# A fused sliding-window attention and gated FFN on one core: seven-product outputs for five tiles instead of two, half-sums formed in place

## The chip, the cores and the metric

One core of a Trainium2 chip. The engines are TensorE (PE, with its weight loads PEld), VectorE (DVE), ScalarE (ACT), GpSimd (POOL) and SyncE (SP), which issues DMAs. The metric is the device time of one launch in microseconds, the median over several runs. The kernel is built with a tile framework that inserts the semaphores; the order of instructions on each engine is the order in which the program emits them.

## The reference

```python
# attention: q, k, v are (8, 8, 576, 64): batch, head, position, head dimension
scores = (1 / sqrt(64)) * matmul(q, k.transpose(0, 1, 3, 2))
mask = (rel >= 0) & (rel < 64)                    # rel = query position - key position
attn = softmax(where(mask, scores, -1e9))
x = matmul(attn, v).transpose(0, 2, 1, 3).reshape(4608, 512)
# gated feed-forward: w_gate and w_val are (512, 1536), w_out is (1536, 512)
out = (maximum(x @ w_gate, 0) * (x @ w_val)) @ w_out
```

## The kernel before

**Tiles.** The 4608 tokens are cut into ten tiles: 0 to 3 of 384 tokens, 4 to 9 of 512 (`NS = 4`, `LAST = 9`). For a wide tile t the program emits a hidden layer (`fast_hidden`) and then an output layer. Between the pieces of tile t's output stand the value products of tile t+1 (`values`: PE products, then on VectorE reciprocal, normalisation and a 32x32-block transpose, "turn") and the scores of tile t+2 (`scores`: PE products, exponentials on ScalarE, masks on VectorE). So attention work runs one and two tiles ahead.

**Seven products.** The hidden layer multiplies 2x2 blocks with seven products instead of eight (Winograd's form). P1 to P7 are accumulated in PSUM banks that ScalarE copies ("snap", "seed") and VectorE adds. For this the kernel needs block differences of the weights, formed once (`us`, `vs`), and of x, formed per tile by `x_form` into `xc` (four per tile: on VectorE up to tile 4, on GpSimd from tile 5 on). A hidden layer works on three groups j = 0, 1, 2 of features.

**Outputs.** Tiles 2 to 6 and 9 use `fast_output`: 48 matmuls of 512 columns for a wide tile. Tiles 7 and 8 (`FAST_OUT`) use `SevenOut`: seven products of 12 matmuls with 256 columns each. These need four half-sums of g, the gated hidden layer (`g_form`, index n = 0 to 3, in three pieces j), and four differences of w_out (`o_form`, 12 instructions). The half-sums of pieces 0 and 1 with n = 0, 1 are made by GpSimd during the hidden layer; of the last piece by VectorE, followed by n = 2 for all pieces on VectorE and n = 3 on GpSimd (behind a small copy, L679, that makes GpSimd wait for VectorE). Their results lie in memory of other tiles that is no longer used: `nats` (raw q and k), `qTs[0]`, `kTs[0]`. P5 uses n = 0, P6 n = 1, P7 n = 2, P3 n = 3.

**Order.** A planner, `Weaver`, holds a clock in estimated microseconds and a heap of due events: `W.at(time, fn)` plans an emission, `W.advance(t)` emits all that is due. PE work advances the clock. An engine's queue is in order and doesn't wait for the planner's time, only for semaphores; the planned time sets the place in the queue. `bank()` hands out one of eight PSUM banks and waits (in the plan) until one is free. Before P3 the add of P7 must have read its bank.

**Loads.** q and k come in by GpSimd-issued DMAs (`qk_load`, batch b) into `nats` and are transposed on VectorE (`qk_trans`, 4 per batch) at planned times within tile t for the scores of tile t+2, which stand at the end of tile t's output; v comes in by GpSimd-issued DMAs (`v_load`) and is copied between partitions by SP-issued ones (`v_spread`). `ahead(t)` plans them for tiles t+2 and t+3, relative to T (the start of tile t) and `ends` (T + 32.7 for a wide tile).

The order within the output of a seven-product tile is a tuple, v for values, s for scores, h for the first product of the next hidden layer:

```python
SEVEN = {-2: ("v0", "P2", "v1", "P6", "P5", "P7", "s0", "P4", "s1", "P3"),
         -1: ("v0", "P2", "P6", "v1", "P7", "P5", "P4", "h1", "P3")}
```

Of the kernel before, what the change touches and what calls it, by code (L numbers as in the profile page):

```python
# [47 lines left out]
def kernel(  # L48
# [10 lines left out]
    nc = tc.nc  # L59
# [31 lines left out]

    wg = persist.tile([128, NC, DF], FP16)
# [219 lines left out]

    def u_pv(u, hhs=(0, 1), banks=None):

        d = units[u]
        if "pv" not in d:
            if u >= 6:
                d["pv"] = [bank() for _ in range(2)]
                unread.update(map(id, d["pv"]))
            elif banks:  # L320
                d["pv"] = [one_bank() for _ in range(2)]
            else:
                d["pv"] = two_banks()
# [12 lines left out]
        return 0.27 * len(hhs)  # L336
# [11 lines left out]
    def u_norm(u, hh):  # L348

        d = units[u]  # L350
        if "x" not in d:
            d["x"] = a_n.tile([128, 2, SB, 2, D // 2], FP16, name="x")
        nc.vector.tensor_tensor(d["x"][:, hh], pv_of(d, u, hh)[:, :, 0:D].rearrange("p s (c e) -> p s e c", e=2),
                                d["r"][:, hh, :, :, None].to_broadcast([128, SB, 2, D // 2]), MUL)
        if u >= 6:
            read(d["pv"][hh], True)

    def u_norm_act(u, hh):

        d = units[u]  # L360
        if "x" not in d:
            d["x"] = a_n.tile([128, 2, SB, 2, D // 2], FP16, name="x")
# [120 lines left out]
    def t_turn(t, hh):  # L483
        dst = xt_tile(t)[:, 2 * hh:2 * hh + 2].rearrange("p e (s c) -> p s e c", c=32)
        nc.vector.transpose(dst, wides[t]["x"][:, hh])

    xcs = {}

    def x_form(t, n):

        HT = widths[t] // 2
        if t not in xcs:
            xcs[t] = x_sb.tile([128, 4, 2, WT // 2], FP16, name="xc", tag="xt")
        xt, xc = xt_tile(t), xcs[t][:, :, :, 0:HT]
        b11, b12, b21, b22 = (xt[:, 2 * k:2 * k + 2, HT * h:HT * h + HT] for k in range(2) for h in range(2))
        x, y = ((b12, b11), (b22, xc[:, 0]), (b22, b12), (b21, xc[:, 1]))[n]
        (nc.vector if t <= NS else nc.gpsimd).tensor_tensor(xc[:, n], x, y, SUB)
        if n == 3:
            normed[0] = t

    def values(t, hh, T, banks=None, give=False):
# [87 lines left out]
    def fast_hidden(t, seven=None):  # L589
# [4 lines left out]
        xt, xc = xt_tile(t), xcs[t][:, :, :, 0:HT]  # L594
# [60 lines left out]
        def add(j, name, i, n, delay):  # L655

            def summed():
# [11 lines left out]
                else:  # L669
                    def product_of():  # L670
                        late = seven and j == last
                        mult(nc.vector if late else nc.gpsimd, j, n, 1, pr[:, 0], pr[:, 1])
                        if seven and n == 0:
                            for s in range(2):
                                g_form(nc.vector if late else nc.gpsimd, t, s, j)
                            if late:
                                for jj in range(3):
                                    g_form(nc.vector, t, 2, jj)
                                nc.gpsimd.tensor_copy(last2[0:1], gsums[2][0:1, HF - 1, 0:2])  # L679
                                for jj in (2, 0, 1):  # L680
                                    g_form(nc.gpsimd, t, 3, jj)
# [57 lines left out]
    def fast_output(t, between):  # L739
# [3 lines left out]
        for sub, before in enumerate(between):  # L743
# [13 lines left out]
            def evac(op=op, sub=sub):  # L757
# [7 lines left out]
    wts = persist.tile([128, 3, HF, QN], FP16)  # L765
    wos = {(k, n): wo[:, HF * k:HF * k + HF, QN * n:QN * n + QN] for k in range(2) for n in range(2)}
    gsums = [nats.rearrange("p a n -> p (a n)")[:, HF * QN * i:HF * QN * i + HF * QN].rearrange("p (f n) -> p f n", f=HF)
             for i in range(3)]
    dead = [tile_.rearrange("p a s c -> p (a s c)")[:, 0:HF * QN].rearrange("p (f n) -> p f n", f=HF)
            for tile_ in (qTs[0], kTs[0])]  # L770
    gsums.append(dead[0])
    wts_ = [dead[1]] + [wts[:, i] for i in range(3)]

    def o_form(eng, n, j):

        c = slice(2 * j, 2 * j + 2)
        to = wts_[n][:, c]
        b11, b12, b21, b22 = (wos[k, m][:, c] for k in range(2) for m in range(2))
        x, y, op = ((b12, b11, SUB), (wts_[2][:, c], b11, ADD), (b22, b12, SUB), (b21, wts_[1][:, c], SUB))[n]
        eng.tensor_tensor(to, x, y, op)  # L780

    def g_form(eng, t, n, j):
# [5 lines left out]
        x, y, op = ((a21, a22, ADD), (gsums[0][:, c], a11, SUB), (a11, a21, SUB), (a12, gsums[1][:, c], SUB))[n]  # L788
        eng.tensor_tensor(gsums[n][:, c], x, y, op)  # L789
        gs[t][1]["sum", n, j] = True  # L790

    class SevenOut:
# [8 lines left out]
        def product(self, name):  # L801
# [10 lines left out]
            f0, h, n = {"P1": (0, 0, None), "P2": (HF, 0, None), "P4": (HF, 1, None)}.get(name, (0, 0, None))  # L812
            s = {"P5": 0, "P6": 1, "P7": 2, "P3": 3}.get(name)
            B = {"P1": wos[0, 0], "P2": wos[1, 0], "P3": wos[1, 1], "P4": wts_[3],
                 "P5": wts_[0], "P6": wts_[1], "P7": wts_[2]}[name]
            for c0, c1 in ((0, 4), (4, 6)):
                for m in range(2):
                    W.advance(W.clock)
                    for c in range(c0, c1):
                        while (("sum", s, c // 2) if s is not None else (f0 + c, h)) not in done:  # L820
                            W.pop()
                        A = gsums[s][:, c] if s is not None else g_sb[:, f0 + c, 256 * h:256 * h + 256]
# [48 lines left out]
        def do_P2(self):  # L871
            self.evac("B", 0, 0)

# [48 lines left out]
    def output_last(t):  # L922
# [3 lines left out]
        for c0, c1, queue in ((0, 256, nc.sync), (256, 384, nc.sync), (384, DM, nc.scalar)):  # L926
# [4 lines left out]
            o_sb = consts.tile([128, c1 - c0], FP32, name=f"o_last{c0}")  # L931
            nc.scalar.copy(o_sb, op[:, 0:c1 - c0])
            queue.dma_start(out[bass.ds(starts[t] + last * 128, 128), c0:c1], o_sb)

    SEVEN_LAST = ("P6", "P5", "P2", "P7", "oP1", "P3", "P4")
    SEVEN = {-2: ("v0", "P2", "v1", "P6", "P5", "P7", "s0", "P4", "s1", "P3"),
             -1: ("v0", "P2", "P6", "v1", "P7", "P5", "P4", "h1", "P3")}

    with tc.manual_schedule():
# [12 lines left out]
        zero32 = consts.tile([128, 384], FP32)  # L952
# [120 lines left out]
        LAST = NS + NL - 1  # L1073
        FAST_OUT = (LAST - 2, LAST - 1)
# [12 lines left out]
        def ahead(t):  # L1087
# [17 lines left out]
        def begin(t):  # L1105
            if t not in running:
                ready(t)
# [19 lines left out]
        for t in range(2, NS + NL):  # L1127
            ready(t)
            ahead(t)
            begin(t)  # L1130
            if t in FAST_OUT:
                seven = sevens[t]
                if t == FAST_OUT[0]:
                    for j in range(3):
                        W.at(W.clock + 0.5, lambda j=j: o_form(nc.gpsimd, 0, j))
# [12 lines left out]
            if t == FAST_OUT[0] - 1:  # L1148
                for i, n in enumerate((2, 1, 3)):
                    for j in range(3):  # L1150
                        W.at(W.clock + 10 + 0.1 * (3 * i + j), lambda n=n, j=j: o_form(nc.gpsimd, n, j))
# [48 lines left out]
```

## Time and profile before

| what | value |
|---|---|
| median of 3 runs | 312.11 us (311.72 to 312.48) |
| profiled execution, its own time | 312.83 us |
| its span, first to last instruction | 311.1 us |
| granted TensorE clock | 1.000 of full speed |
| tile 2 and tile 3, hidden start to hidden start | 24.58 and 26.59 us |
| tile 9, from its second group of products to the end | 30.95 us |
| GpSimd TENSOR_TENSOR `g_sb<-pr`, 128x512, f32 to f16 (mean) | 1.27 us |
| GpSimd TENSOR_TENSOR `nats<-g_sb`, 128x512 f16 (mean) | 1.15 us |
| VectorE TENSOR_TENSOR `pr<-bank,pr`, 128x512 f32 (mean) | 0.68 us |
| VectorE transposes of q, k and of x (mean) | 1.25 us |
| loads of v (128 KB) and of q (288 KB), issue to landing | 5.5 and 7.2 us |

The span starts with the first instruction of any engine. A row of the profile's groups or timeline names the engine, the line of the program, the operation, then what is written and read; "x3" counts instructions, and what stands in brackets is idle time before it and what ended it. Where a helper issues an instruction, the helper's line stands there: L625 is every hidden product, L754 the normal output, L823 the seven-product output, L431 the masks, L497 the x differences, L789 the half-sums of g, L780 the differences of w_out, L198 the transposes of q and k, L485 those of x, L479 the normalisation, L650 the products of gate and value, L661 the adds in the hidden layer, L864 the adds in the output.

### The profile page before, as it was taken

The numbers are of one execution on the slowest core, as the hardware profiler recorded it, in microseconds if no ns is written. First come the engines' busy times: TensorE is split into PE (matmuls) and PEld (weight loads), VectorE is DVE, ScalarE is ACT, GpSimd is POOL, SyncE is SP. The second block draws the span as 40 slices with busy tenths as digits, with TensorE's granted clock in tenths as the row PEclk, the third lists the DMA queues.
The fourth block names the chain that finished last, engine by engine and source line by source line (L and its number), as shares of the span: only waits on it lengthen the run. The fifth ranks groups of instructions, "written<-read, shape, count | busy, mean of one in ns | idle before, by whom it ended". The sixth has DMA issues, their size and how long they took to land.

```text
span 311.1 us, 10718 instructions
## 1 busy us (share of the span) xinstructions
PE 297.2 (96%) x4511; PEld 226.6 (73%) x4511; DVE 239.8 (77%) x460; ACT 198.1 (64%) x410; POOL 194.1 (62%) x222
## 2 busy tenths in 40 slices
PE   4899989999999998999999999999999999999996
PEld 2575878449958955885588558855888788878854
DVE  5937976987997999689868986898559986885540
ACT  3645348158858845982888278837885688537842
POOL 8768689849930491237924792999873927483430
PEclk9999999999999999999999999999999999999999
DMA  7999996999994189304990399011910210012012
GB/s 218 183 196 205 194 193 104 135 194 165 75 187 131 39 140 188 76 0 66 223 154 1 44 231 158 7 36 70 152 32 16 69 59 0 3 55 84 1 37 101
DMA packets 57169, 32.84 MB, mean 106 GB/s; under 512 B 39456, under 2 KB 49568, under 8 KB 57120
## 3 DMA queue, kind: packets, MB, share of 16 engines
q0 software_dynamic: 46688, 18.29, 50.1%
q1 hardware_dynamic: 10288, 13.80, 14.0%
q8 instruction: 35, 0.57, 0.7%
q14 instruction: 14, 0.11, 0.1%
q10 hardware_dynamic: 144, 0.07, 0.1%
HBM read 37.75 MB, written 9.44 MB: 152 GB/s over the span
## 4 chain that ended last, share of the span: by engine, by line
PE 79%; DVE 7%; DMA 5%; POOL 4%; issue 3%; ACT 1%; DVEq 0%; POOLq 0%
PE bank L625 42%; PE bank L754 18%; PE bank L897 5%; PE bank L580 5%; PE bank L264 3%; DMA wg<-in_moe_w_gate_dram 3%; PE bank L823 2%; DMA v<-in_v_dram 2%; PE bank L460 2%; DVE xw L479 1%; POOL v L204 1%; DVE nats L789 1%; PE bank L332 1%; DVE g_sb L650 1%; PE bank L929 1%
## 5 line engine op out<-in xcount | busy, mean ns | idle before, releaser
L650 POOL TENSOR_TENSOR g_sb<-pr 128x512 f16<-128x512 f32 (+1 forms) x44 | 52.6, 1206 | 74.9 <-ACT pr L667 73.3
L661 DVE TENSOR_TENSOR pr<-bank,pr 128x512 f32<-128x512 f32 (+1 forms) x96 | 58.6, 650 | 4.8 <-PE bank L625 3.3
L754 PE MATMUL bank<-wo,g_sb 128*128 128x512 f16 x252 | 58.0, 380 | 1.3 <-issue 1.3
L644 ACT COPY pr<-bank 128x512 f32<-128x512 f32 (+1 forms) x96 | 49.3, 567 | 14.5 <-PE bank L625 14.1
L650 DVE TENSOR_TENSOR g_sb<-r,bank 128x512 f16<-128x512 f32 (+1 forms) x48 | 31.4, 653 | 29.4 <-ACT r L690 22.6
L754 PEld LDWEIGHTS <-g_sb 128*128 128x128 f16 x252 | 23.2, 98 | 27.7 <-issue 1.9
L625 PE MATMUL bank<-xc,vs 128*128 128x256 f16 (+1 forms) x288 | 41.3, 266 | 0.1
L625 PE MATMUL bank<-xc,us 128*128 128x256 f16 (+1 forms) x288 | 41.3, 266 | 0.0
L625 PEld LDWEIGHTS <-vs 128*128 128x128 f16 x384 | 36.5, 98 | 3.9 <-issue 0.4
L625 PEld LDWEIGHTS <-us 128*128 128x128 f16 x384 | 36.5, 98 | 3.3
L204 POOL DMA_DIRECT2D v<-in_v_dram x41 | 34.7, 864 | 1.7 <-DMA nats<-in_q_dram 1.0
L759 ACT COPY o_sb<-bank 128x512 f32<-128x512 f32 x21 | 12.3, 587 | 32.6 <-PE bank L754 30.6
L431 DVE TENSOR_TENSOR pw<-pw,mask 128x512 f16<-128x512 f16 x48 | 28.6, 633 | 5.2 <-ACT pw L426 4.4
L667 ACT ACTIVATE pr<-pr 128x512 f32<-128x512 f32 (+1 forms) x48 | 29.2, 608 | 4.7 <-DVE pr L661 4.7
L690 ACT ACTIVATE r<-bank 128x512 f32<-128x512 f32 (+1 forms) x48 | 27.8, 579 | 5.6 <-PE bank L625 5.4
L625 PEld LDWEIGHTS <-wg 128*128 128x128 f16 x288 | 27.4, 98 | 3.9 <-issue 0.2
L625 PEld LDWEIGHTS <-wv 128*128 128x128 f16 x288 | 27.4, 98 | 2.5
L625 PE MATMUL bank<-xt,wv 128*128 128x256 f16 (+1 forms) x192 | 27.5, 266 | 0.0
L625 PE MATMUL bank<-xt,wg 128*128 128x256 f16 (+1 forms) x192 | 27.5, 266 | 0.0
L426 ACT ACTIVATE pw<-bank 128x512 f16<-128x512 f32 x48 | 24.9, 605 | 1.8 <-PE bank L264 1.2
L634 ACT COPY bank<-bank 128x512 f32<-128x512 f32 (+1 forms) x48 | 24.9, 553 | 0.6 <-PE bank L625 0.4
L563 ACT ACTIVATE pr<-bank 128x384 f32<-128x384 f32 x24 | 11.5, 493 | 16.2 <-PE bank L580 13.2
(106 smaller groups left out, 517.2 us busy)
## 6 DMA issues: line engine op xcount, KB each, us to landing
out_dram<-o_sb SPq DMA_DIRECT2D x35, 256.0 KB, 3.3
nats<-in_k_dram POOLq DMA_DIRECT2D x15, 288.0 KB, 5.3
nats<-in_q_dram POOLq DMA_DIRECT2D x15, 288.0 KB, 7.2
v<-in_v_dram POOLq DMA_DIRECT2D x31, 128.0 KB, 5.5
v<-v SPq DMA_DIRECT2D x12, 132.0 KB, 2.5
v<-v SPq DMA_DIRECT2D x24, 66.0 KB, 2.1
wg<-in_moe_w_gate_dram POOLq DMA_DIRECT2D x6, 256.0 KB, 6.5
wv<-in_moe_w_val_dram POOLq DMA_DIRECT2D x6, 256.0 KB, 8.3
```

The costliest lines, as they stand in the source:

```text
L204: nc.gpsimd.dma_start(v16s[b % 2][lo:hi, g, :, 0:64], v[b, :, 64 * g - 64 + lo:64 * g - 64 + hi].rearrange("h p d -> p h d"))
L426: nc.scalar.activation(d["p"][g].rearrange("p n c -> p (n c)"), d["st"][g], ACT.Exp, scale=scale)
L431: nc.vector.tensor_tensor(d["p"][g], d["p"][g], mask[:, None, :].to_broadcast([128, 2 * QW, 64]), MUL)
L580: nc.tensor.matmul(h[:, b * n:b * n + n], wt[:, c, (f + b) * 128:(f + b) * 128 + 128], xt[:, c, c0:c0 + n], start=(c == 0), stop=(c == NC ...
L625: nc.tensor.matmul(to[:, HT * m:HT * m + HT], w[:, k, 128 * m:128 * m + 128], x[:, k], start=(first and m == 0 and k == 0), stop=(k == 1), ...
L634: nc.scalar.copy(at[j, "B", i][:, 0:TW], at[j, "A", i][:, 0:TW])
L644: nc.scalar.copy(pr[:, i], at[j, "A", i][:, 0:TW])
L650: eng.tensor_tensor(gh[:, f:f + 2, h], pair(r), pair(v), MUL)
L661: nc.vector.tensor_tensor(pr[:, i], to[:, 0:TW], pr[:, i], ADD)
L667: nc.scalar.activation(pr[:, 0], pr[:, 0], ACT.Relu)
L690: nc.scalar.activation(r, to[:, 0:TW], ACT.Relu)
L754: nc.tensor.matmul(op, g_sb[:, f, 128 * sub:128 * sub + 128], wo[:, f], start=(i == 0), stop=(i == NF - 1))
```

## The change

Five tiles (4 to 8) use `SevenOut` instead of two. The half-sums of g no longer need four buffers: n = 0 is written over a block of g, n = 2 and n = 3 over others, and only n = 1 has a buffer of its own, `s2`, which shares memory with the x tile of the narrow tiles (`xus`). The differences of w_out get four buffers of their own and are formed by GpSimd in tiles 3 and 4 (six each) instead of 6 and 7. In tiles 4 to 7 VectorE makes n = 2 of the last piece only and GpSimd the other two; n = 3 follows on GpSimd, planned behind P2. The x differences of tiles 5 to 9 move from GpSimd to VectorE and are planned together behind P4. P5 takes the bank that has been free longest. Transposes of q and k, loads of q, k and v get other planned times; GpSimd waits at two places for masks (`behind_quad`). In tile 8 the second turn is planned 0.8 us later and the next tile's first product no longer waits in the plan for the x differences.

```diff
+    xus = persist.tile([128, 2, 2, U // 32 * D], FP16)
...
+    def behind_quad(qd):
+        nc.gpsimd.tensor_copy(last[0:1], quads[qd]["p"][G - 1][0:1, QW, 0:2])
...
-        (nc.vector if t <= NS else nc.gpsimd).tensor_tensor(xc[:, n], x, y, SUB)
+        (nc.vector if t <= NS or t - 1 in FAST_OUT else nc.gpsimd).tensor_tensor(xc[:, n], x, y, SUB)
...
-    def values(t, hh, T, banks=None, give=False):
+    def values(t, hh, T, banks=None, give=False, turn=2.7):
...
-        W.at(T + 0.7, lambda: t_recip(t, hh))
+        W.at(T + (1.15 if give else 0.7), lambda: t_recip(t, hh))
...
-        W.at(T + 2.7, lambda: t_turn(t, hh))
-        for n, x in (((0, 4.0),), ((1, 4.0), (2, 4.1), (3, 5.0)))[hh]:
+        W.at(T + turn, lambda: t_turn(t, hh))
+        for n, x in (((0, 4.0),), ((1, 4.0), (2, 4.1), (3, 5.0)))[hh] if not give else ():
...
                             if late:
-                                for jj in range(3):
+                                masks = t + 2 <= LAST
+                                for jj in (j,) if masks else range(3):
                                     g_form(nc.vector, t, 2, jj)
-                                nc.gpsimd.tensor_copy(last2[0:1], gsums[2][0:1, HF - 1, 0:2])
-                                for jj in (2, 0, 1):
-                                    g_form(nc.gpsimd, t, 3, jj)
+                                nc.gpsimd.tensor_copy(last2[0:1], g_sb[0:1, HF - 1, 0:2])
+                                for jj in range(2) if masks else ():
+                                    g_form(nc.gpsimd, t, 2, jj)
...
-    wts = persist.tile([128, 3, HF, QN], FP16)
+    wts = persist.tile([128, 4, HF, QN], FP16)
...
+    s2 = xus.rearrange("p a h n -> p (a h n)")[:, 0:HF * QN].rearrange("p (f n) -> p f n", f=HF)
...
-        x, y, op = ((a21, a22, ADD), (gsums[0][:, c], a11, SUB), (a11, a21, SUB), (a12, gsums[1][:, c], SUB))[n]
-        eng.tensor_tensor(gsums[n][:, c], x, y, op)
+        to, x, y, op = ((a21, a21, a22, ADD), (s2[:, c], a21, a11, SUB), (a11, a22, s2[:, c], SUB), (a12, a12, s2[:, c], SUB))[n]
+        eng.tensor_tensor(to, x, y, op)
...
-                at[self.TO[name]] = bank()
+                at[self.TO[name]] = bank(0, name == "P5")
...
         def do_P2(self):
             self.evac("B", 0, 0)
+            for j in range(3):
+
+                def formed(j=j):
+                    while ("sum", 2, 2) not in gs[self.t][1]:
+                        W.pop()
+                    g_form(nc.gpsimd, self.t, 3, j)
+                W.at(W.clock + 1.0, formed)
...
+    FAST_OUT = (LAST - 5, LAST - 4, LAST - 3, LAST - 2, LAST - 1)
+    O_FORMS = {3: [(1.5 + 0.1 * j, 2, j) for j in range(3)] + [(1.8, 0, 0), (6.5, 0, 1), (9.0, 0, 2)],
+               4: [(2.5 + 0.1 * i, n, j) for i, (n, j) in enumerate((n, j) for n in (1, 3) for j in range(3))]}
+    LATE, VAT, QAT = (6.0, 8.0, 10.7, 14.2), 1.0, 4.0
+    XAT = -0.3
...
-                qk_turns(t + 2, T, (0.1, 1.4, 8.0, 14.2) if long else (0.1, 1.4, 6.1, 10.7))
-                v_ahead(t + 2, ends, ends - 5.0 if long else T + 3.0 if t == 2 else ends + 0.5)
+                qk_turns(t + 2, T, LATE if t - 1 in FAST_OUT else (0.1, 1.4, 8.0, 14.2) if long else (0.1, 1.4, 6.1, 10.7))
+                v_ahead(t + 2, ends, ends + VAT if t in FAST_OUT else ends - 5.0 if long else T + 3.0 if t == 2 else ends + 1.5)
+                if t + 1 == NS:
+                    W.at(ends + 1.4, lambda: behind_quad(3))
             if t + 3 <= LAST:
-                qk_loads(t + 3, ends - 11.0)
+                qk_loads(t + 3, ends - (QAT if t in FAST_OUT else 11.0))
...
+            if t == 3:
+                behind_quad(1)
+            for T, n, j in O_FORMS.get(t, ()):
+                W.at(W.clock + T, lambda n=n, j=j: o_form(nc.gpsimd, n, j))
             if t in FAST_OUT:
...
                     if name[0] == "v":
-                        values(t + 1, int(name[1]), W.clock, [bank(0, True) for _ in range(3)], True)
+                        values(t + 1, int(name[1]), W.clock, [bank(0, True) for _ in range(3)], True,
+                               3.5 if t == LAST - 1 else 2.7)
...
                     elif name[0] == "h":
+                        while ("turned", 0) not in wides[t + 1]:
+                            W.pop()
                         begin(t + 1)
                     else:
                         seven.product(name)
+                        if name == "P4":
+                            for n in range(4):
+                                W.at(W.clock + XAT + 0.05 * n, lambda n=n: x_form(t + 1, n))
```

More of the change, by code (lines that the diff above doesn't have):

```diff
@@ L361, in u_norm_act @@
         if "x" not in d:
-            d["x"] = a_n.tile([128, 2, SB, 2, D // 2], FP16, name="x")
+            d["x"] = xus[:, u % 2].rearrange("p h (s e c) -> p h s e c", e=2, c=D // 2)
         pv = pv_of(d, u, hh)
@@ L764 @@
     QN = DM // 2
-    wts = persist.tile([128, 3, HF, QN], FP16)
+    wts = persist.tile([128, 4, HF, QN], FP16)
     wos = {(k, n): wo[:, HF * k:HF * k + HF, QN * n:QN * n + QN] for k in range(2) for n in range(2)}
[L767 to L772, printed above, removed]
+    s2 = xus.rearrange("p a h n -> p (a h n)")[:, 0:HF * QN].rearrange("p (f n) -> p f n", f=HF)
     def o_form(eng, n, j):
         c = slice(2 * j, 2 * j + 2)
-        to = wts_[n][:, c]
+        to = wts[:, n, c]
         b11, b12, b21, b22 = (wos[k, m][:, c] for k in range(2) for m in range(2))
-        x, y, op = ((b12, b11, SUB), (wts_[2][:, c], b11, ADD), (b22, b12, SUB), (b21, wts_[1][:, c], SUB))[n]
+        x, y, op = ((b12, b11, SUB), (wts[:, 2, c], b11, ADD), (b22, b12, SUB), (b21, wts[:, 1, c], SUB))[n]
         eng.tensor_tensor(to, x, y, op)
@@ L821, in product @@
                             W.pop()
-                        A = gsums[s][:, c] if s is not None else g_sb[:, f0 + c, 256 * h:256 * h + 256]
+                        A = s2[:, c] if name == "P6" else g_sb[:, f0 + c, 256 * h:256 * h + 256]
                         nc.tensor.matmul(to[:, QN * m:QN * m + QN], A[:, 128 * m:128 * m + 128], B[:, c],
@@ L951 @@
             v_fixed(i, nc.vector)
-        zero32 = consts.tile([128, 384], FP32)
+        zero32 = wts.rearrange("p a f n -> p (a f n)").bitcast(FP32)[:, 0:384]
         nc.vector.memset(zero32, 0.0)
```

36 lines of the change are left out of this document (16 added, 20 removed).

## The prediction, written before the changed kernel was run

> **What bounds the kernel now.** I read the page's busy times and its chain of waits first, to learn which engine sets the end.
>
> ```profile
> PE 297.2 (96%) x4511; PEld 226.6 (73%) x4511; DVE 239.8 (77%) x460; ACT 198.1 (64%) x410; POOL 194.1 (62%) x222
> PE 79%; DVE 7%; DMA 5%; POOL 4%; issue 3%; ACT 1%; DVEq 0%; POOLq 0%
> L754 PE MATMUL bank<-wo,g_sb 128*128 128x512 f16 x252 | 58.0, 380 | 1.3 <-issue 1.3
> ```
>
> TensorE sets the end; only fewer columns on it, or fewer holes, can shorten the run. The next view is the table by stage, one row per 512-row tile, cut where the chain starts the next tile's hidden layer (tiles 4 to 8; the last row also holds 0.87 us of tile 9's first products).
>
> ```profile
> 122.31:154.02 31.71, 31.71 (x474) 23.21 (x473) 26.64 (x45) 22.05 (x42) 17.22 (x17) 1.00 0.44 96
> 154.02:185.74 31.72, 31.72 (x475) 23.23 (x473) 26.66 (x45) 22.06 (x42) 18.96 (x20) 1.00 0.69 108
> 185.74:217.50 31.76, 31.76 (x474) 23.25 (x473) 26.78 (x44) 22.06 (x42) 25.48 (x24) 1.00 0.46 71
> 217.50:249.00 31.50, 30.95 (x511) 26.76 (x509) 23.93 (x43) 22.32 (x43) 23.05 (x23) 1.00 0.47 67
> 249.00:280.15 31.15, 30.33 (x390) 26.41 (x389) 24.52 (x48) 20.53 (x39) 17.50 (x16) 1.00 0.09 29
> ```
>
> The columns are length, then busy time of PE, PE's loads, DVE, ACT and POOL. Tiles 4 to 6 have no hole on PE and give DVE 26.7 us of work in 31.7. Tile 7, which has the seven products already, is only 0.26 shorter than tile 6. The last view is the timeline of tile 7's output, and beside it what a mask costs next to GpSimd.
>
> ```profile
> 239.32 0.42 DVE L789 TENSOR_TENSOR nats<-g_sb 128x512 f16<-128x512 f16 x1
> 240.13 1.08 DVE L789 TENSOR_TENSOR nats<-g_sb 128x512 f16<-128x512 f16 x3
> 241.13 1.34 DVE L479 TENSOR_TENSOR xw<-bank,rw 128x128 f16<-128x128 f32 x3
> 241.41 3.37 POOL L789 TENSOR_TENSOR qT<-g_sb,nats 128x512 f16<-128x512 f16 x3
> 241.47 1.47 PE L823 MATMUL bank<-kT,nats 128*128 128x256 f16 x12 [0.21 <-DVE xw L479]
> 246.85 4.34 DVE L431 TENSOR_TENSOR pw<-pw,mask 128x512 f16<-128x512 f16 x5
> 278.68 1.47 PE L823 MATMUL bank<-wo,qT 128*128 128x256 f16 x12 [0.59 <-DVE o_sb L864]
> 148.91 1.33 POOL L497 TENSOR_TENSOR xc<-xt 128x512 f16<-128x512 f16 x1
> 151.49 4.26 POOL L204 DMA_DIRECT2D v<-in_v_dram  x5
> L431 DVE TENSOR_TENSOR pw<-pw,mask 128x512 f16<-128x512 f16 x2 | 2.7, 1371 | 0.0
> L431 DVE TENSOR_TENSOR pw<-pw,mask 128x512 f16<-128x512 f16 x2 | 0.8, 424 | 0.1
> 252.88 0.69 DVE L650 TENSOR_TENSOR g_sb<-r,bank 128x512 f16<-128x512 f32 x1
> ```
>
> The two mask rows are from 149.8 to 150.6, with GpSimd's x differences running, and from 152.8 to 153.5, with GpSimd only issuing loads of v: 1.37 us against 0.42. An fp16 operation of VectorE on two SBUF tiles costs 0.95 more beside a GpSimd sum and nothing more beside GpSimd's DMA issues.
>
> **The products, part one.** A normal wide output is 48 matmuls of 512 columns; the chain has 2.70 us for 12, so 10.80. Seven products are 84 of 256 columns; the chain has 1.31 for 12, so 9.17. Each of tiles 4, 5 and 6 could give 1.63, 4.9 together. Tile 7 shows how much of it stays. In PE starts, from its P1 (233.93) to tile 8's first product (248.84) there are 14.91 us; work in it is 9.17 for products, 1.75 for four hidden pieces (0.436 each), 1.24 for two value and 1.24 for two score groups, together 13.40. 1.5 us are holes. So the question is what the new order does to the holes.
>
> **The output phase redrawn, on tile 7's times.** (1) VectorE formed five half-sums from 239.32 to 241.21; now it forms three (two of index 0 and 1, one of index 2), so it is free at 240.55, 0.66 earlier. Normalisation and turns, which follow, move up by as much: the first value bank comes free 0.6 earlier. (2) P5 waited from 241.08 to 241.47 for such a bank; it now takes the longest-free bank and need not wait. It ends at 242.4. (3) New wait: P7 needs the index-2 sums of the other two pieces, made by GpSimd behind a small copy that waits for VectorE (0.17, as at 241.27). At 1.13 each (3.37 for three) they end at about 243.0; P7's first matmuls can start on piece 0, so about 0.4 is lost. Queued behind P7 on PE are the scores. (4) Those needed a normalised bank at 244.53; it is now free by 243.98, when P7 ends at 244.16, so that hole of 0.4 closes. (5) P4 and the second scores follow; the latter still wait some 0.25 for the third exponential. (6) P3 needs the index-3 sums; GpSimd makes them right behind, 243.0 to 246.4, and P3 starts at 247.2. It needs the add of P7 too: VectorE's second turn ends near 245.7, the add 246.3. P3 ends at 248.5 instead of 248.84: **0.35 saved**, a stage of 31.15.
>
> The form of these sums is new: they write into strided g. Nearest rows are 1.15 (strided source) and 1.27 (the fp32 multiplication into g) on GpSimd; below, 1.12. I take 1.13 because sizes and type are those of the first. At 1.27, P7 is 0.25 later per tile, 1.2 over five tiles; at 1.12 nothing changes.
>
> **x differences.** Four leave GpSimd (1.25 each, 244.75 to 250.24) for VectorE, where tile 4's took 0.42, spaced 0.34. In the new order they come behind P7's add and one mask, from about 246.7, when GpSimd's sums end at 246.4. Uncontended they cost VectorE 1.5. The eight masks gain: before, five took 0.87 each beside GpSimd's differences; now most take 0.42. VectorE's queue (add, 4 differences, 8 masks, last add) ends about 3.2 us into the next tile; before it ended 3.9 in, and the first gate product was due right then (252.88, against 249.00). Cover left: 0.7. Bounds for the four: 1.4 to 5.5; I take 1.5.
>
> **Tiles 4 to 6** carry what tile 7 does not: four transposes of 1.22 (4.9). VectorE had 26.7 there; two late multiplications (1.25), three half-sums (1.15), two adds (1.25) and four differences (1.5) add 5.15, uncontended masks take off some 2.5 (5.1 to 6.5 before, 3.3 at 0.42): 29.3 in a stage of 31.15. It fits, with 6% to spare. The moved transposes (6.0, 8.0, 10.7, 14.2 us) fall into idle times of tile 7's hidden layer of 0.69, 1.13, 0.43 and 2.02; so gate products slip by up to 1.75 and catch up by the last slot. The banks they free are wanted about as late; I put 0.1 on it, bounds 0 and 1.2.
>
> Tile 4 is worse. GpSimd now waits there for the masks (about 122.2), then issues v loads (4.3) and makes six weight differences (1.16 each) until 133.5, so its first multiplication slips from 129.6 to 133.5 and its sums end at 143.1, under VectorE's first late multiplication. I add 0.4. The six differences in tile 3 lie in its idle GpSimd time (12.8 us before 101.31). Later q and k loads (four issues of 0.56) and v loads (0.86 each) come right behind the index-3 sums, land some 7 us after, and are first needed 6 us into the next tile; GpSimd's first multiplication is due at 7.2, so they cost nothing unless that cover of about 2 us goes. SP's v copies wait for them, but the next store is due 21 us into the tile.
>
> **Tile 8.** P3 waited from 277.93 to 278.68 for P7's add, which stood behind a 1.25 us turn. That turn now comes at 3.5 instead of 2.7, behind the add: **0.75 saved**. The differences follow the turn, the first by 279.05, and tile 9 wants it at 279.24. Without it 0 is saved.
>
> **Sum.** Tile 4 0.2, tile 5 0.5, tile 6 0.5, tile 7 0.35, tile 8 0.75: 2.3 us. The profiled execution took 312.83 (span 311.1 and 1.7 around it), so it would be 310.5; the median of the runs is 0.72 lower, so **309.8**. One stall I leave at zero: 1.31 us at 116.45 in tile 3, which the profile puts down to nothing, while DMA queues were full and v loads were being issued. These loads now come 9 us later; the stall may go, or another may appear elsewhere: plus or minus 1.3.
>
> **Rivals.** *More is regained.* The redrawing is pessimistic: holes close in all five tiles. Against 13.40 of work, another half microsecond in each and the stall at 116.45 gone gives 2.3 + 2.5 + 1.3 = 6.1, so 306.0. For it: bank holes were what tile 7 mostly showed. Against it: P7's new wait.
>
> *GpSimd's sums meet VectorE's differences: slower.* If the index-3 sums run 0.7 us or more later than drawn, differences and masks run beside them. Three caught operations cost 3 x 0.95 = 2.85; less the cover of 0.7, the first gate product of tiles 5 to 8 is 2.15 late and PE runs out of banks: 8.6 in four tiles, less 2.3 gained, so 316 (the break-even lies at 1.3 caught operations per tile). For it: the margin between 246.4 and 246.7 is thin. Against it: one order on both engines ties the sums to VectorE's own earlier work. The Trainium skill, "SBUF — State Buffer", Who interferes with whom, says that a VectorE instruction with two SBUF inputs and a GpSimd one that reads SBUF exclude each other, whoever starts first holding it for the whole instruction. By that rule every operation that meets a sum waits it out, as the 1.37 us row shows.
>
> *VectorE is full: no change.* If masks stay at their 5.1 to 6.5, VectorE needs 31.8 in tiles 4 to 6, as long as the stages are now. Those tiles give nothing, tiles 7 and 8 give 1.1 less a little for late transposes: 311.5.
>
> **Chances.** Forecast 0.52 (its own range 308.3 to 311.2), more regained 0.19, collision 0.17, VectorE full 0.12. A measurement of this kernel tells about 0.2%, 0.6 us, from no change. The forecast and the larger gain are faster; the full VectorE lies on the edge and gives 0.09 to same. Faster 0.73, same 0.1, slower 0.17. The range takes in the larger gain and the full VectorE and leaves out most of the collision: 305.8 to 313.0.
>
> **What would show it.** Stages of tiles 4 to 7 near 31.1 and of tile 8 near 30.4; P7 waiting for GpSimd some 0.4; x differences at 0.42 on VectorE; the first gate product of a tile no later than 3.9 in; no wait of P3 in tile 8. The forecast is wrong if differences or masks show above 0.8, or if PE has holes in the hidden layers of tiles 4 to 6.

## The result, and the profile after

The changed kernel takes 309.95 us (median, 309.41 to 310.46) against 312.03 us (311.72 to 312.48) for the kernel before: a ratio of 0.9932, 95% interval 0.9909 to 0.9955. The forecast was 309.8. The profiled execution took 309.65 with a span of 308.0, 3.1 less than before.

First the page of the changed kernel, its busy times and the shares of its chain of waits.

```profile
PE 294.9 (96%) x4619; PEld 237.0 (77%) x4619; DVE 245.0 (80%) x499; ACT 200.3 (65%) x413; POOL 196.4 (64%) x230
PE 74%; issue 7%; POOL 7%; DVE 4%; DMA 4%; ACT 3%; SPq 0%; POOLq 0%; DVEq 0%; ACTq 0%
```

TensorE still sets the end, with 2.3 us less busy time; VectorE has 5.2 more. Next the table by stage of the changed kernel, cut as before, at the start of the hidden layer of tiles 4 to 8 and of the rest of tile 9 (length, then busy time of PE, its loads, DVE, ACT, POOL).

```profile
121.68:153.28 31.60, 31.12 (x510) 26.70 (x509) 27.43 (x50) 22.32 (x43) 28.96 (x30) 1.00 0.47 57
153.28:184.45 31.17, 31.01 (x510) 26.73 (x509) 28.85 (x57) 22.74 (x44) 21.80 (x24) 1.00 0.72 111
184.45:215.63 31.18, 31.01 (x511) 26.75 (x509) 28.86 (x57) 22.75 (x44) 21.82 (x22) 1.00 0.73 116
215.63:246.81 31.18, 30.93 (x511) 26.69 (x509) 24.83 (x53) 22.74 (x44) 17.28 (x17) 1.00 0.50 76
246.81:277.00 30.19, 30.14 (x390) 26.41 (x389) 23.91 (x50) 20.60 (x39) 13.20 (x12) 1.00 0.10 34
```

Against the rows of before the five stages lose 0.11, 0.55, 0.58, 0.32 and 0.96 us. Tile 4 stands out: GpSimd (last of the five) is busy 29 of 31.6 us there. Last, the timeline of tile 7's output in the changed kernel, with the first gate product of tile 8 and P3 of tile 8. Lines of the changed kernel have higher numbers: L633 is every hidden product, L763 the normal output, L827 the seven-product output, L435 the masks, L505 the x differences, L793 the half-sums of g, L784 the differences of w_out, L483 the normalisation, L658 the products of gate and value, L868 the adds in the output.

```profile
238.24 0.42 DVE L793 TENSOR_TENSOR g_sb<-g_sb,xus 128x512 f16<-128x512 f16 x1
238.84 1.30 DVE L483 TENSOR_TENSOR xw<-bank,rw 128x128 f16<-128x128 f32 x3
238.87 5.60 POOL L793 TENSOR_TENSOR g_sb<-g_sb,xus 128x512 f16<-128x512 f16 x5
239.30 1.69 PE L827 MATMUL bank<-wts,g_sb 128*128 128x256 f16 x14
241.18 1.27 PE L827 MATMUL bank<-wts,g_sb 128*128 128x256 f16 x10 [0.18 <-POOL g_sb L793]
242.38 0.68 PE L265 MATMUL bank<-qT,kT 32*128 32x64 f16 x64
244.97 0.41 DVE L505 TENSOR_TENSOR xc<-xt 128x512 f16<-128x512 f16 x1
246.43 1.76 DVE L435 TENSOR_TENSOR pw<-pw,mask 128x512 f16<-128x512 f16 x5
250.69 0.69 DVE L658 TENSOR_TENSOR g_sb<-r,bank 128x512 f16<-128x512 f32 x1 [1.24 <-ACT r L699]
275.53 1.47 PE L827 MATMUL bank<-wo,g_sb 128*128 128x256 f16 x12
```

GpSimd's five sums follow VectorE's one; at 241.18 P7's last ten matmuls wait for them. The wait is 0.35 us from start to start (0.46 between two matmuls that else start 0.11 apart); the row's 0.18 counts from the end that the profile models for the matmul before. The x differences (0.41) and five masks (0.35 each, against 0.87 before) run when GpSimd has no sum left. The first gate product waits for ScalarE, not for VectorE, and P3 of tile 8 waits for nothing.

### The profile page after: what moved, and what is told of

It reads as the page before. It is cut to its first block, busy times and chain, and to the rows that moved or that the text cites. A ratio compares the mean times of both kernels' runs of the same rounds, so it can differ in the third digit from the quotient of the medians.

```text
span 308.0 us, 10983 instructions
## 1 busy us (share of the span) xinstructions
PE 294.9 (96%) x4619; PEld 237.0 (77%) x4619; DVE 245.0 (80%) x499; ACT 200.3 (65%) x413; POOL 196.4 (64%) x230
## 4 chain that ended last, share of the span: by engine, by line
PE 74%; issue 7%; POOL 7%; DVE 4%; DMA 4%; ACT 3%; SPq 0%; POOLq 0%; DVEq 0%; ACTq 0%
PE bank L633 41%; PE bank L827 9%; PE bank L588 8%; PE bank L763 8%; POOL g_sb L793 4%; DMA out_dram<-o_sb 3%; PE bank L265 3%; PE bank L908 3%; POOL xus L793 2%; DVE qT L199 2%; PE bank L336 1%; DMA vs<-in_k_dram 1%; ACT o_sb L858 1%; DVE kT L199 1%; PE bank L940 1%
## 5 line engine op out<-in xcount | busy, mean ns | idle before, releaser
L658 POOL TENSOR_TENSOR g_sb<-pr 128x512 f16<-128x512 f32 (+1 forms) x38 | 45.0, 1195 | 48.5 <-ACT pr L675 48.3
L658 DVE TENSOR_TENSOR g_sb<-r,bank 128x512 f16<-128x512 f32 (+1 forms) x48 | 31.2, 650 | 25.9 <-ACT r L699 23.5
L633 PE MATMUL bank<-xc,us 128*128 128x256 f16 (+1 forms) x288 | 41.3, 266 | 0.3 <-ACT bank L642 0.3
L633 PE MATMUL bank<-xc,vs 128*128 128x256 f16 (+1 forms) x288 | 41.3, 266 | 0.1
L633 PEld LDWEIGHTS <-vs 128*128 128x128 f16 x384 | 36.5, 98 | 4.3 <-issue 0.4
L633 PEld LDWEIGHTS <-us 128*128 128x128 f16 x384 | 36.5, 98 | 3.8 <-issue 0.4
L827 PEld LDWEIGHTS <-g_sb 128*128 128x128 f16 x360 | 34.0, 98 | 6.6 <-POOL g_sb L793 1.7
L633 PEld LDWEIGHTS <-wg 128*128 128x128 f16 x288 | 27.4, 98 | 3.3 <-issue 0.2
L633 PEld LDWEIGHTS <-wv 128*128 128x128 f16 x288 | 27.4, 98 | 2.5
L633 PE MATMUL bank<-xt,wg 128*128 128x256 f16 (+1 forms) x192 | 27.5, 266 | 0.0
L633 PE MATMUL bank<-xt,wv 128*128 128x256 f16 (+1 forms) x192 | 27.5, 266 | 0.0
L793 POOL TENSOR_TENSOR g_sb<-g_sb,xus 128x512 f16<-128x512 f16 x23 | 25.7, 1144 | 0.0
L763 PE MATMUL bank<-wo,g_sb 128*128 128x512 f16 x108 | 24.8, 380 | 0.4 <-issue 0.4
L827 PE MATMUL bank<-wo,g_sb 128*128 128x256 f16 x180 | 22.4, 273 | 0.2 <-DVE g_sb L658 0.2
L827 PE MATMUL bank<-wts,g_sb 128*128 128x256 f16 x180 | 21.8, 273 | 0.8 <-POOL g_sb L793 0.4
```

What stands on the lines that cost most here:

```text
L633: nc.tensor.matmul(to[:, HT * m:HT * m + HT], w[:, k, 128 * m:128 * m + 128], x[:, k], start=(first and m == 0 and k == 0), stop=(k == 1), ...
L658: eng.tensor_tensor(gh[:, f:f + 2, h], pair(r), pair(v), MUL)
L763: nc.tensor.matmul(op, g_sb[:, f, 128 * sub:128 * sub + 128], wo[:, f], start=(i == 0), stop=(i == NF - 1))
L827: nc.tensor.matmul(to[:, QN * m:QN * m + QN], A[:, 128 * m:128 * m + 128], B[:, c], start=(first and m == 0 and c == 0), stop=(c == HF - 1 ...
```

## The experiments

Each is the changed kernel with one statement edited (early_turns sets two values in it); forms_in_t3 has the edit of late_mult_gpsimd and one more. "Stage" is from TensorE's first hidden product of a tile to that of the next, in the profiled execution. "Tile 8" here ends at tile 9's first product, which stands ahead of P3. The ratio is to the kernel before, run on the same chip.

| kernel | median us | ratio (95%) | tile 3 | tile 4 | tile 5 | tile 6 | tile 7 | tile 8 |
|---|---|---|---|---|---|---|---|---|
| before | 312.03 | 1 | 26.59 | 31.71 | 31.71 | 31.77 | 31.50 | 28.21 |
| changed | 309.95 | 0.9932 (0.9909 to 0.9955) | 25.45 | 31.60 | 31.18 | 31.18 | 31.18 | 28.00 |
| two_tiles | 311.32 | 0.9956 (0.9931 to 0.9981) | 25.75 | 31.71 | 31.83 | 31.69 | 31.11 | 28.01 |
| all_sums_vector | 312.27 | 1.0001 (0.9980 to 1.0022) | 25.48 | 32.14 | 31.70 | 31.71 | 31.71 | 28.00 |
| x_on_gpsimd | 311.38 | 0.9972 (0.9955 to 0.9990) | 26.02 | 31.59 | 32.17 | 31.58 | 31.43 | 28.28 |
| late_mult_gpsimd | 309.23 | 0.9906 (0.9877 to 0.9936) | 26.29 | 32.18 | 30.91 | 30.91 | 30.88 | 27.87 |
| early_loads | 311.43 | 0.9956 (0.9937 to 0.9974) | 25.77 | 32.34 | 31.94 | 31.18 | 31.18 | 28.01 |
| early_turns | 312.21 | 1.0001 (0.9976 to 1.0026) | 25.77 | 32.74 | 31.88 | 31.36 | 31.17 | 28.01 |
| loads_in_idle | 311.95 | 0.9970 (0.9944 to 0.9995) | 25.47 | 32.71 | 31.88 | 31.61 | 31.17 | 28.01 |
| turn_first_t8 | 311.35 | 0.9959 (0.9935 to 0.9983) | 25.77 | 31.59 | 31.18 | 31.17 | 31.19 | 28.01 |
| v_first_t3 | 309.69 | 0.9914 (0.9898 to 0.9929) | 26.55 | 31.11 | 31.17 | 31.18 | 31.19 | 28.00 |
| late_mult_5_to_8 | 309.08 | 0.9885 (0.9849 to 0.9921) | 25.52 | 31.60 | 30.91 | 30.91 | 30.88 | 27.87 |
| forms_in_t3 | 308.20 | 0.9838 (0.9800 to 0.9876) | 25.66 | 30.82 | 30.91 | 30.90 | 30.88 | 27.86 |

The stages of tiles 5 to 8 repeat within 0.02 us where nothing touches them, so they show a tenth of a microsecond; medians don't, as the first 96 us of the profiled executions alone vary by 3 us (tile 3 starts between 95.2 and 98.4).

**two_tiles: where do the microseconds come from?**

```diff
-    FAST_OUT = (LAST - 5, LAST - 4, LAST - 3, LAST - 2, LAST - 1)
+    FAST_OUT = (LAST - 2, LAST - 1)
```

> The changed kernel, but seven products only in tiles 7 and 8; tiles 4 to 6 use the normal output, with their x differences on GpSimd and their loads and transposes at the old times. Theory (the gain of tiles 4 to 6 is that of the products, the gain of tiles 7 and 8 that of their new order): tiles 4 to 6 go back to 31.7 us each, from 31.60, 31.17 and 31.18; tiles 7 and 8 stay near 31.2 and 30.2; the time rises by 1.2 us against the changed kernel. Rival (tiles 7 and 8 gain only because of what tiles 4 to 6 hand on): tiles 7 and 8 also go back, to 31.5 and 31.15, and the time rises by 2.5 us.

Tiles 4 to 6 go back to 31.7 to 31.8, tiles 7 and 8 keep their gain. The stages from tile 4 on add up to 1.2 more (0.11 + 0.65 + 0.51 - 0.07 + 0.01). So the switch of tiles 4 to 6 to seven products, with the x differences, loads and transposes that go back with it, brings 1.2 us; tiles 7 and 8 gain by their own order.

**all_sums_vector: is the new wait of P7 a loss?**

```diff
-                                masks = t + 2 <= LAST
+                                masks = False
```

> In tiles 4 to 7 VectorE makes all three pieces of the index-2 sums, so P7 doesn't wait for GpSimd. Rival (the wait of P7, 0.35 us a tile, is a pure loss): the time falls by 1.4 us. Theory (that wait is covered, because the scores behind P7 start only when the normalisation frees their bank, at 242.36 in tile 7, and P7 ends at 242.3): VectorE reaches the normalisation 0.66 us later, the scores start about 0.65 us later, each of tiles 4 to 7 is 0.4 to 0.65 us longer, and the time rises by 1.6 to 2.6 us.

Tiles 4 to 7 are each 0.52 to 0.54 longer; the rival falls. The timeline of its tile 7 shows the two waits that come instead.

```profile
241.32 1.09 DVE L793 TENSOR_TENSOR g_sb<-g_sb,xus 128x512 f16<-128x512 f16 x3
242.57 1.30 DVE L483 TENSOR_TENSOR xw<-bank,rw 128x128 f16<-128x128 f32 x3
242.87 2.78 PE L827 MATMUL bank<-wts,g_sb 128*128 128x256 f16 x24 [0.21 <-DVE xw L483]
246.12 0.66 PE L265 MATMUL bank<-qT,kT 32*128 32x64 f16 x61 [0.34 <-DVE xw L483]
```

VectorE makes three index-2 sums in a row. P5 and then the scores wait for banks that its normalisation (L483) frees. GpSimd's share of the sums is what pays in tiles 4 to 7, and the 0.35 us that P7 waits for it is covered: the scores need the bank that the second 128x448 normalisation of the second value group frees. Here that one ends at 246.07 and the scores go on at 246.12; in the changed kernel it ends at 242.33 and they start at 242.38, just as P7 is done.

**x_on_gpsimd: the x differences back on GpSimd.**

```diff
-        (nc.vector if t <= NS or t - 1 in FAST_OUT else nc.gpsimd).tensor_tensor(xc[:, n], x, y, SUB)
+        (nc.vector if t <= NS else nc.gpsimd).tensor_tensor(xc[:, n], x, y, SUB)
```

> The x differences of tiles 5 to 9 are back on GpSimd, behind its sums. Theory: they take 1.3 us each there and run from 244.45 to 249.8 (tile 7's times) beside the masks, which go from 0.42 to 1.37 us while they do; VectorE ends its queue about 5 us into the next tile instead of 2.7, the first gate product comes 1.1 us late in tiles 5 to 9, GpSimd's first multiplication 2 us late in tiles 5 and 6; the time rises by 1 to 4 us. Rival (moving the differences is neutral, as GpSimd has time): within 0.5 us.

The timeline at the turn from tile 5 to tile 6 (which starts at 185.77):

```profile
183.55 1.16 POOL L505 TENSOR_TENSOR xc<-xt 128x512 f16<-128x512 f16 x1
187.25 1.33 POOL L505 TENSOR_TENSOR xc<-xt,xc 128x512 f16<-128x512 f16 x1
183.76 5.78 DVE L435 TENSOR_TENSOR pw<-pw,mask 128x512 f16<-128x512 f16 x6
190.73 0.67 DVE L658 TENSOR_TENSOR g_sb<-r,bank 128x512 f16<-128x512 f32 x1
```

Six masks take 5.78 us where five took 1.76, and the first gate product comes 4.96 us into the tile instead of 4.04. The stages pay 0.99, 0.40, 0.25 and 0.28 in tiles 5 to 8; in tile 5 a transpose also waits 0.61 us for k, issued later. Moving the differences is not neutral.

**late_mult_gpsimd: is VectorE's chain the bound in the output?**

```diff
-                        mult(nc.vector if late else nc.gpsimd, j, n, 1, pr[:, 0], pr[:, 1])
+                        mult(nc.vector if late and n == 0 else nc.gpsimd, j, n, 1, pr[:, 0], pr[:, 1])
```

> The first of VectorE's two late products of gate and value (0.6 us at 234.8 in tile 7) goes to GpSimd, which idles from 234.8 to 238.7. Theory (VectorE's chain to the half-sums and the normalisation sets P7 and the scores): everything behind it on VectorE moves up by about 0.4 us, the wait of P7 closes, tiles 5, 6 and 7 get 0.3 to 0.4 us shorter, tile 8 0 to 0.2, tile 4, where GpSimd is late, 0 to 0.4 longer: the time falls by 0.6 to 1.6 us. Rival (TensorE waits for ScalarE's copies and exponentials there): within 0.3 us.

In its tile 7 P5 and P7 run without a stop:

```profile
239.29 2.84 PE L827 MATMUL bank<-wts,g_sb 128*128 128x256 f16 x24
```

Tiles 5 to 7 fall by 0.27 to 0.30, tile 8 by 0.13; tile 4 grows by 0.58, more than the 0 to 0.4 expected, so the five stages together fall by 0.39 only, less than the 0.6 to 1.6 of the theory. The scores of tile 7 start 9.94 us after the first output product, against 10.24 (242.06 less 232.12; 242.38 less 232.14), again 0.05 behind the normalisation, which ends at 242.01. VectorE's chain is the bound there: it sets P7's sums and the scores' bank.

**early_loads: GpSimd's sums made to meet VectorE's differences**, the slower rival of the prediction.

```diff
-    LATE, VAT, QAT = (6.0, 8.0, 10.7, 14.2), 1.0, 4.0
+    LATE, VAT, QAT = (6.0, 8.0, 10.7, 14.2), 1.0, 11.0
```

> The q and k loads of tiles 4 and 5 are planned 7 us earlier, which puts their four issues (2.25 us) on GpSimd between its index-2 and its index-3 sums; nothing else differs. So the index-3 sums come 2.25 us later than in the changed kernel and meet VectorE's differences and first masks, as the slower rival of the prediction had it. Theory (the collision is real, its price smaller than drawn, since about 1.2 us of VectorE's lateness is covered at the start of a tile): differences and one mask go from 0.42 to 1.2 to 1.4 us, P3 waits up to 1 us for the sums, tiles 4 and 5 are 0.8 to 1.5 us longer each, the time rises by 1.6 to 3 us. Rival (there is slack enough, the order of loads is of no account): within 0.4 us.

The timeline at the end of its tile 4:

```profile
149.73 3.62 POOL L793 TENSOR_TENSOR g_sb<-g_sb,xus 128x512 f16<-128x512 f16 x3
151.09 1.25 DVE L435 TENSOR_TENSOR pw<-pw,mask 128x512 f16<-128x512 f16 x1
152.26 1.37 DVE L505 TENSOR_TENSOR xc<-xt 128x512 f16<-128x512 f16 x1
153.40 0.61 PE L827 MATMUL bank<-wo,g_sb 128*128 128x256 f16 x4 [0.47 <-POOL g_sb L793]
157.90 0.69 DVE L658 TENSOR_TENSOR g_sb<-r,bank 128x512 f16<-128x512 f32 x1 [0.19 <-ACT r L699]
```

The index-3 sums come 2.2 us late; one mask and one difference are caught (1.25 and 1.37), and P3's last four matmuls wait (0.63 us from start to start). Tiles 4 and 5 pay 0.74 and 0.76, a little below the expected 0.8 to 1.5. VectorE is late, but the first gate product comes 4.05 us into the tile as ever, and still waits for ScalarE: the loss is P3's.

**early_turns: the transposes back at their old times**, with loads early enough for them.

```diff
-    LATE, VAT, QAT = (6.0, 8.0, 10.7, 14.2), 1.0, 4.0
+    LATE, VAT, QAT = (0.1, 1.4, 8.0, 14.2), 1.0, 13.0
```

> The transposes of q and k in tiles 5 and 6 are back at 0.1, 1.4, 8.0 and 14.2 us; their loads are issued earlier, in GpSimd's idle time before the index-2 sums, so that they are there. Theory: VectorE's queue at the start of these tiles is 2.45 us longer and ends at 5.1 instead of 2.65 us; the first gate product, due at 3.88, is 1.2 us late, and TensorE loses 0.3 to 1 us in each of the two tiles: the time rises by 0.6 to 2 us. Rival (the banks that product frees are not wanted so early, and VectorE catches up): within 0.3 us.

Tiles 4, 5 and 6 grow by 1.14, 0.70 and 0.18. But tile 4 has no early transpose, so this run could not be read as planned; in tile 4 ScalarE waits 2.0 us for an output store. It called for the next run.

**loads_in_idle: the early loads alone.**

```diff
-    LATE, VAT, QAT = (6.0, 8.0, 10.7, 14.2), 1.0, 4.0
+    LATE, VAT, QAT = (6.0, 8.0, 10.7, 14.2), 1.0, 13.0
```

> Only the q and k loads of tiles 4 and 5 are moved, into GpSimd's idle time before the index-2 sums, 8 us earlier than in the changed kernel; the transposes stay late. It separates the two edits of early_turns, whose tile 4 grew by 1.1 us before any early transpose came, with ScalarE waiting 2.0 us for an output store to free its buffer. Theory (the transfers of q and k hold up the output stores, and those the buffers of ScalarE's copies): tile 4 again 32.7 us, tile 5 about 31.7, tile 6 31.18, the time up by 1.2 to 2 us. Rival (tile 4's loss was something else of that run): tiles 4 and 5 as in the changed kernel, the time within 0.4 us.

Tiles 4 and 5 grow as much without the early transposes (1.11 and 0.70). ScalarE's waits from 120 to 190 us of this kernel, total, times and longest:

```profile
ACT o_sb L841 <- DMA out_dram<-o_sb: 2.5, 2, 1.9
```

The changed kernel has no such wait in that window. Issued 8 us earlier, q and k are moved while the first output store is. That store, issued at 144.43, lands after 8.48 us, against 3.31 in the changed kernel; one of three output buffers comes free late, and the copy that empties P4's bank waits for it. Tile 6 grows too, by 0.43, which was not expected: the same copy of tile 5 waits 0.54 us for a store, and 4 us later TensorE waits 0.33 us for ScalarE. What the early transposes cost is what early_turns has over this run: none that shows (tile 6 31.36 against 31.61, both with late stores), though the gate product was 0.85 us later there (4.89 into the tile) than in the changed kernel.

**turn_first_t8: the second turn of tile 8 ahead of P7's add.**

```diff
-                        values(t + 1, int(name[1]), W.clock, [bank(0, True) for _ in range(3)], True,
-                               3.5 if t == LAST - 1 else 2.7)
+                        values(t + 1, int(name[1]), W.clock, [bank(0, True) for _ in range(3)], True,
+                               2.7)
```

> In tile 8 the second turn is planned at 2.7 again, ahead of the add of P7. Theory: P3 waits for that add again, 0.75 to 0.8 us, and the time rises by as much; all else stays. Rival (P3 waits for ScalarE or for the sums anyway): within 0.2 us.

P3 waits again; the row of its timeline:

```profile
279.14 1.47 PE L827 MATMUL bank<-wo,g_sb 128*128 128x256 f16 x12 [0.81 <-DVE o_sb L868]
```

Tiles 4 to 8 are those of the changed kernel. From tile 9's first product to the end it takes 34.26 us against 33.30: 0.96 more, where 0.75 to 0.8 was expected. The ratio is 0.0027 higher, 0.8 us, which the intervals alone would not settle.

**v_first_t3: v loads of tile 3 ahead of GpSimd's wait for the masks.**

```diff
-                v_ahead(t + 2, ends, ends + VAT if t in FAST_OUT else ends - 5.0 if long else T + 3.0 if t == 2 else ends + 1.5)
+                v_ahead(t + 2, ends, ends + VAT if t in FAST_OUT else ends - 5.0 if long else T + 3.0 if t == 2 else ends + 0.5)
```

> In tile 3 GpSimd issues the v loads before it waits for the masks instead of behind that wait, so at about 114 instead of 121.8 us; the six weight differences follow the wait at about 121.4 instead of 126. Theory (tile 4 gives little because GpSimd comes 4.3 us late into it): tile 4 goes from 31.60 to 31.2 us. On tile 3 the run tells two readings of the 1.31 us stall of the kernel before apart: if the v loads beside TensorE's stream cause it, tile 3 goes from 25.45 back to some 26.5 us and the time rises by 0.4 to 0.9; if not, tile 3 stays and the time falls by 0.4.

The timelines of TensorE and GpSimd in tile 3; the last two rows are the same five matmuls in the kernel before and in the changed one:

```profile
113.23 4.28 POOL L205 DMA_DIRECT2D v<-in_v_dram  x5
114.72 1.68 PE L763 MATMUL bank<-wo,g_sb 128*128 128x512 f16 x7
117.68 1.24 PE L763 MATMUL bank<-wo,g_sb 128*128 128x512 f16 x5 [1.28 <-issue]
117.76 1.24 PE L754 MATMUL bank<-wo,g_sb 128*128 128x512 f16 x5 [1.31 <-issue]
117.13 1.24 PE L763 MATMUL bank<-wo,g_sb 128*128 128x512 f16 x5 [0.20 <-issue]
```

Tile 4 falls to 31.11, as the theory has it. A stall of 1.28 us stands behind the seventh matmul again, and tile 3 is at 26.55. But the reading that the loads alone cause it doesn't hold: all eleven other profiled kernels here, with the late loads, stop at the same matmul, for 0.20 to 1.03 us (0.20 in the changed kernel, 1.03 in late_mult_gpsimd, 0.47 in the middle). The two with early loads have the two longest stops, 1.31 and 1.28. That the loads lengthen it is likely, with two against eleven; what TensorE waits for there is taken up in the last section. In the medians the two effects of this edit leave no difference.

**late_mult_5_to_8 and forms_in_t3: versions that go further.** The first takes tile 4 out of late_mult_gpsimd, the second keeps it in and moves three weight differences to tile 3.

```diff
-                        mult(nc.vector if late else nc.gpsimd, j, n, 1, pr[:, 0], pr[:, 1])
+                        mult(nc.vector if late and (n == 0 or t == FAST_OUT[0]) else nc.gpsimd, j, n, 1, pr[:, 0], pr[:, 1])
```

> late_mult_gpsimd, but not in tile 4, where GpSimd was late and the move cost 0.58 us. Theory: tile 4 back at 31.6, tiles 5 to 8 as in late_mult_gpsimd (30.91, 30.91, 30.88, 0.13 less in tile 8), the time 0.9 to 1.0 us below the changed kernel and 0.5 below late_mult_gpsimd. Rival (what tile 4 lost, tile 5 gained): no difference from late_mult_gpsimd.

```diff
-               4: [(2.5 + 0.1 * i, n, j) for i, (n, j) in enumerate((n, j) for n in (1, 3) for j in range(3))]}
+               4: [(2.5 + 0.1 * j, 3, j) for j in range(3)]}
+    O_FORMS[3] += [(19.0 + 0.1 * j, 1, j) for j in range(3)]
```

> late_mult_gpsimd in all five tiles, and three of tile 4's six weight differences moved to GpSimd's idle time at 114 us in tile 3. Theory (tile 4 loses only by GpSimd's lateness): GpSimd is 3.4 us earlier in tile 4, which falls from 32.18 to 31.0; tile 3 pays up to 1 us if the three meet VectorE's x differences and masks (each operation caught costs 0.95). The time is 0.5 to 1.3 us below late_mult_5_to_8 if they don't. Rival (they are caught and TensorE waits): tile 3 longer by as much as tile 4 gains.

Tile 4 is back at 31.60 in the first and at 30.82 in the second. In the second the three differences of w_out meet one x difference of tile 3:

```profile
114.32 3.39 POOL L784 TENSOR_TENSOR wts<-wts,wo 128x512 f16<-128x512 f16 x3
115.59 2.42 DVE L505 TENSOR_TENSOR xc<-xt 128x512 f16<-128x512 f16 x1
```

That one takes 2.42 instead of 0.42, and tile 3 grows by 0.2 at most (25.66 against 25.45 to 25.52). Tiles 4 to 8 together take 0.98 us less than in the changed kernel in the first (0.9 to 1.0 expected) and 1.76 less in the second. The ratio of forms_in_t3, 0.9838 (0.9800 to 0.9876), lies wholly below that of the changed kernel; the interval of late_mult_5_to_8 it overlaps, and there the stages tell.

## Why the prediction was right

**The sum.** Forecast for tiles 4 to 8: 0.2, 0.5, 0.5, 0.35 and 0.75, together 2.3. Measured: 0.11, 0.55, 0.58, 0.32 and 0.96, together 2.5. The products themselves would give 1.63 a tile; two_tiles shows that 1.2 for three tiles is what stays. The rest goes into holes, as drawn from tile 7: its output takes 14.51 us for 13.40 of work. The late transposes, on which 0.1 was put, cost nothing that shows: tiles 5 and 6, which have them, are as long as tile 7, which has none. Outside these tiles the profiled execution has 1.1 less in tile 3, where the stall of 1.31 shrank to 0.20 (the term that was left at plus or minus 1.3), and 0.7 more in tile 2, which the edits hardly reach and which lies between 24.58 and 25.56 in these kernels. The stall's share is not all the change's: tile 3 of the kernels with the late loads has stops up to 1.03. That 309.8 lies 0.15 from the median is luck: the interval alone is 0.7 us to each side, and the profiled execution, at 309.65, is 0.85 below its own forecast of 310.5.

**The output phase.** From P1 to the next tile it is 14.51 us in tile 7; drawn were 14.56. P7's wait is 0.35 (0.4 drawn), the scores follow at once, P3 waits for nothing. One step had the wrong cause: P5's wait was to go because P5 takes the bank that is longest free. With that edit undone the program is the same, instruction for instruction, banks included, so it can't have moved anything; that the wait went all the same was luck. P5 finds its bank because VectorE is earlier, and all_sums_vector shows it waiting again when VectorE is late. Also, the 0.4 that P7 "loses" was booked as a loss; it is covered by the normalisation that the scores wait for.

**x differences and masks.** Forecast: 1.5 us for four, masks at 0.42, VectorE's queue ending 3.2 us into the next tile. In tile 7 four run in 1.5 (244.97 to 246.51), masks at 0.35 spacing, and the queue ends 2.65 in (249.46 against 246.81). VectorE's load of tiles 5 and 6, forecast 29.3, is 28.9. The form of the sums written into g: 5.60 for five, 1.12 each, where 1.13 was taken.

**Tile 4.** The lateness of GpSimd was seen (sums until 143.1 forecast, 142.97 measured), and 0.4 set on it. v_first_t3 gives 0.49, and the late multiplication in tile 4, at 140.76, takes 1.19 instead of 0.69.

**Tile 8.** 0.75 forecast for the turn; from tile 9's first product to the end the time falls by 0.77 (34.07 to 33.30), and turn_first_t8 gives 0.96 back. The other 0.2 lie in P6: before, its last four matmuls wait 0.17 us for VectorE's sums (271.84), now they don't. The reciprocals stand behind the last late multiplication now and so bring those sums forward; no run undoes that edit alone.

**The rivals.** The collision is real but was priced too high, at 2.15 us a tile: early_loads, with sums 2.2 us late and two operations caught, costs 0.75. Its total was also added up wrongly: 8.6 lost less 2.3 gained is 6.3 above the 312.1 of before, so 318.4; 316 takes the 2.3 off twice. The failing step is the last one, that PE loses what the first gate product is late. early_turns and x_on_gpsimd have that product 0.85 and 0.9 late in tile 6, which pays 0.18 and 0.40: less than half of it. In early_loads it is P3's wait for the sums that costs. The lock that the Trainium skill describes ("SBUF — State Buffer", Who interferes with whom) fits the caught rows, 1.25 to 1.37 us. The 2.42 us row starts at 115.59 and ends 0.3 behind the last of the three weight differences (117.71), so it looks held over two GpSimd operations; how the two engines take turns no run isolates. A full VectorE did not happen, because masks fell to 0.42 and below. That more is regained did not happen by itself, but late_mult_5_to_8 and forms_in_t3 show that about 0.3 us was to be had in each of tiles 5 to 7, and from VectorE's chain.

**Loads.** "They cost nothing" holds for the late places that they have. The reason given, GpSimd's cover, was half of it: loads_in_idle shows that an earlier place, free on GpSimd, costs 1.8 us in tiles 4 and 5, and 0.4 in tile 6, through the output stores.

## What to carry to other kernels

Where one stage of the old kernel already runs the new scheme, redraw that stage instruction by instruction and carry its holes over: that gave 0.5 a tile here, and 0.55 and 0.58 were measured, where counting matmuls gave 1.63. Before removing a wait of the bounding engine, find what the instruction behind it waits for; if that is as late, the wait is free, and work must leave the engine that sets both. A place for a load is judged by what the transfers meet, not only by the issuing engine's idle time.

## What the runs showed of the hardware that was not expected

TensorE stops without a cause that the profile names, always behind the seventh of twelve matmuls of the same output in tile 3, for 0.20 to 1.31 us in thirteen profiled kernels, longest (1.31 and 1.28) in the two where v loads are in flight beside it. Ten of them also stop at the like place in tile 2, for 0.20 to 0.78.

The traces say what it very likely waits for: its own instructions. The page of the kernel before lists 35 packets in a DMA queue "q8 instruction", 0.57 MB; TensorE's 9022 matmuls and weight loads make 258 for each, so the queue looks like TensorE's. The two stops stand behind its 1502nd and 1886th matmul in every kernel that has them. That is 384 matmuls with as many weight loads, three times 256, or about three packets. In tile 3 a packet of that queue ends 1.2 to 1.6 us before TensorE goes on in all thirteen, however long it stood. And the later the packet starts, the longer the stop: the packet starts 0.39 us before the first of the twelve matmuls in the changed kernel (0.20 us lost), 0.49 behind it in late_mult_gpsimd (1.03), 0.64 in v_first_t3 (1.28) and 0.73 in the kernel before (1.31). What makes a packet start late, the v loads or another thing, no run isolates.

An output store of 256 KB that is issued while loads of q and k are under way lands late, after 8.48 us instead of 3.31, and stops ScalarE for 1.9 us, though SyncE issues the store and GpSimd the loads. The loads themselves take no longer beside it (4.3 to 8.2 us, against 5.0 to 10.1 in the changed kernel).
